# Sliding-window attention and two feed-forward layers on one core: both batches' first groups in packed float32, fewer chunks beside the attention, weight splits in step with the products

## The chip, the cores and the metric

One core of a Trainium2 chip runs the program. The metric is the time of one execution on the device in microseconds (us). Three runs of the kernel before gave 637.86, 638.09 and 638.39 us; the median is 638.09 us.

## What is computed

```python
scores = scale * np.matmul(q, k.transpose(0, 1, 3, 2))      # 2 batches, 8 heads, 768 rows, depth 64
keep = (pos[None, :] < n_sink) | ((rel >= 0) & (rel < window))   # n_sink 4, window 128
a = softmax(np.where(keep, scores, -1e9))
x = heads_side_by_side(np.matmul(a, v))                     # 1536 x 512
h = x @ w_in;  x = np.maximum(0.01 * h, h) @ w_out          # first layer, d_ff 2048
h = x @ w_in2; y = (h * sigmoid(h)) @ w_out2                # second layer, d_ff 2048
```

Everything is held to float32 accuracy. The products of the layers are made of three products of split operands (a high and a low part each).

## The kernel before

**Attention.** A unit is one group of 256 query rows (`G`, three groups in each of two batches) and one pair of heads (`p`, four pairs); there are 24 units, and each has two slots of 128 query rows. A slot goes through `scores` (PE makes the products `sc` for head 0 and head 1, DVE masks them into `P`, ACT takes the exponential and its row sum into `sm`), `normalise` (DVE forms the reciprocal of the sum, then `P` is multiplied by it: the first 16 slots on ACT, `ON_ACT`, the others on DVE), and `transposes` (PE transposes `P` with the identity matrix `ident` into `tr` or a bank lent by `h`, ACT copies it to `pT`). `values` multiplies by the values `v` into `at` (in places a bank lent by `ya`), and ACT and DVE split the result into `xh` and `xl`, the input of the layers. Groups after the first of a batch also carry the four sink columns (`psink`, `sink_t`, `sk`) and have 260 columns a head; the first group has 128 columns in slot 0 and 256 in slot 1.

The units of the first `WHOLE` = 2 groups (G = 0 and 1, both of batch 0) take the scores in plain float32, one head after the other; GpSimd fills the upper 64 partitions of their buffers with zeros once, and the loads bring 64 partitions. All later units split queries and keys in two parts first: ACT writes `qkh`, GpSimd `ql`, DVE the lower part of the keys.

**Layers.** `d_ff` is cut in 16 chunks of 128 for each layer. The first `NA` = 6 chunks of the first layer are done beside the attention, group by group, 256 columns wide: `item_h` makes `h` with 12 products, ACT and DVE make `ga` of it, `item_y` makes 12 products into `ya`. That is 36 items. The rest (chunks 6 to 15, and all of the second layer) comes after in passes of 4 and 6 chunks over the three blocks of 512 tokens (`T`), 512 columns wide (`fused_h`, `fused_y`): 78 items of 24 products.

**Weights.** They come as 64-bit words (`wr`), half a chunk in a transfer. `load_half` turns a half into a high and a low part: two ACT instructions (`wb`, `w` or `we`) and five DVE instructions.

**Order.** All of this is recorded first (`Recorder.add`), each instruction with an estimated cost and what it depends on; `Recorder.order` then plays the engines through with these costs and a due time, and issues each engine's instructions in the order that comes out. On the chip each engine keeps that order. The order in which the main loop asks for the work is the rank; `W_FIRST` and `W_EVERY` say from which slot on a half is asked for, and `go` which item goes with a slot.

Of the kernel before, what the change touches and what calls it, by code (L numbers as in the profile page):

```python
# [21 lines left out]
WHOLE = 2  # L22

NA, NE = 6, 4

AHEAD, FETCH = 2, 2

W_FIRST, W_EVERY = 1, 0.9

ON_ACT = 16  # L30
# [76 lines left out]
class Op:  # L107
    def __init__(self, eng, rank):
        self.eng, self.rank = eng, rank
        self.calls, self.cost, self.deps, self.opens, self.users = [], 0, {}, [], []  # L110
        self.bytes, self.port = 0, False


class Recorder:
# [27 lines left out]
    def cost(self, eng, name, out, ins, kw):  # L142
        n = out.size() if isinstance(out, View) else 0
        psum = any(isinstance(a, View) and a.tile.pool.psum for a in [out, *ins])
        if eng == "tensor":
            passes = 4 if ins[0].dtype == F32 else 1

            half = name == "matmul" and out.box[0][1] - out.box[0][0] <= 64
# [5 lines left out]
        if eng == "scalar":  # L154
            return (51 if psum else 93) + n / 1.2 + (186 if "accum_out" in kw else 0)
# [22 lines left out]
    def add(self, eng, name, args, kw):  # L178
# [18 lines left out]
        op.port = op.port or self.shared(eng, out, ins)  # L197
        op.cost += self.cost(eng, name, out, ins, kw)
        if name == "dma_start":
            side = writes[0] if writes else reads[0]  # L200
            op.bytes = 128 * side.size() * 4
        for views, write in ((reads, False), (writes, True)):
            for v in views:
                self.touch(op, v, write)

# [57 lines left out]
    def order(self):  # L263
# [6 lines left out]
        free = dict.fromkeys(self.ENGINES, 0.0)  # L270
        dma = port = 0.0
        ready = {e: [o for o in self.ops if o.eng == e and not o.need] for e in self.ENGINES}
# [27 lines left out]

        while len(done) < len(self.ops):
            best = None
            for e in self.ENGINES:
                can = []
                for o in ready[e]:
                    at = max(o.est, free[e], port if o.port else 0.0)
# [10 lines left out]
                if best is None or (start, o.due) < best[:2]:  # L317
                    best = (start, o.due, o)
            start, _, op = best
            op.start = start  # L320
            if op.bytes:
                free[op.eng] = start + (500 if op.eng == "sync" else 100)
                dma = max(dma, start + 1200) + max(op.bytes / 350.0, 370)
                end = dma + 300
            else:
                end = free[op.eng] = start + op.cost
                if op.port:
# [12 lines left out]
            for u in op.users:  # L340
                u.est = max(u.est, (op.start if not u.deps[op] else end + self.lag(op, u)))
                u.need -= 1
                if not u.need:
                    ready[u.eng].append(u)
# [45 lines left out]
def attention_moe(ctx, tc, cfg, ins, out):  # L390
# [141 lines left out]
    units = [(G, p) for G in range(B * NG) for p in range(NP)]  # L532
    state, sinks = {}, {}

    def load_qk(n):
# [5 lines left out]
        whole = G < WHOLE  # L541
        d = state[n] = dict(G=G, p=p, g=g, whole=whole, nb=2 if g == 0 else 3)
        raw = qk_raw[n % (4 if whole else 2)]

        rows = slice(0, D if n == 0 else P)
        load = slice(0, D if whole else P)
        for j in (slice(0, 1), slice(1, 2)) if n == 0 else (slice(0, 2),):
            R.sync.dma_start(out=raw[load, j, :GT + kw], in_=qkd[n][load, j, :GT + kw])
        if whole:
            d.update(q=[raw[rows]], k=raw[rows, :, GT:])  # L550
            return
        hi = attn.tile([P, 2, GT + 388], F32R, "qkh", 2)
# [7 lines left out]
    def load_v(n):  # L560
# [5 lines left out]
        R.sync.dma_start(out=d["v"][:, :nb], in_=vd[n][:, :nb])  # L566
# [14 lines left out]
    def scores(s):  # L581
# [9 lines left out]
        sm = attn.tile([P, 4], F32, "sm", 4)  # L591
        for j in range(2):
            sc = ps_a.tile([P, 260], F32, "sc", 2)
            with R.group():
                for a, q in enumerate(u["q"]):
                    R.tensor.matmul(sc[:, :nm], q[:, j, i * QB:(i + 1) * QB], u["k"][:, j, k0:k0 + nm],
                                    start=a == 0, stop=a == len(u["q"]) - 1)
# [6 lines left out]
    def normalise(s):  # L604
# [20 lines left out]
    def transposes(s):  # L625
# [101 lines left out]
    n_items = B * NG * NA  # L727
# [224 lines left out]
```

## Time and profile before

| | |
|---|---|
| time of the profiled execution | 638.0 us |
| its span (first to last instruction) | 636.0 us |
| median of three runs | 638.09 us |
| PE busy | 616.7 us (97%) |
| DVE busy | 406.3 us (64%) |
| ACT busy | 335.5 us (53%) |
| GpSimd (POOL) busy | 32.9 us (5%) |
| DMA | 54.39 MB |

The page shows the span in slices; a busy PE is one whose pipelined products leave no gap, not one at its peak. The granted TensorE clock of all slices is 1.0. How far a busy PE is from its pace is read from starts of products in the timeline. Tile names are the kernel's own; every instruction of the recorded part has the line of the issuing loop (L375 before), so that rows are told apart by tiles.

### The profile page before, as it was taken

The numbers are of one execution on the slowest core, as the hardware profiler recorded it, in microseconds if no ns is written. First come the engines' busy times: TensorE is split into PE (matmuls) and PEld (weight loads), VectorE is DVE, ScalarE is ACT, GpSimd is POOL, SyncE is SP. The second block draws the span as 40 slices with busy tenths as digits, with TensorE's granted clock in tenths as the row PEclk, the third lists the DMA queues.
The fourth block names the chain that finished last, engine by engine and source line by source line (L and its number), as shares of the span: only waits on it lengthen the run. The fifth ranks groups of instructions, "written<-read, shape, count | busy, mean of one in ns | idle before, by whom it ended". The sixth has DMA issues, their size and how long they took to land.

```text
span 636.0 us, 9261 instructions
## 1 busy us (share of the span) xinstructions
PE 616.7 (97%) x3392; PEld 521.4 (82%) x3392; DVE 406.3 (64%) x999; ACT 335.5 (53%) x802; POOL 32.9 (5%) x41
## 2 busy tenths in 40 slices
PE   7877899999999999999999999999999999999997
PEld 5566889999999888888888888888888888888886
DVE  4899989887649998693414999239542353333254
ACT  6999998898866654452323674356222242222221
POOL 5001112222000000000000000000000000000000
PEclk9999999999999999999999999999999999999999
DMA  8855535433003444142000343004100000000013
GB/s 223 230 170 179 174 117 189 157 111 109 26 1 133 166 165 164 46 155 99 2 0 1 118 148 113 20 1 146 54 0 1 0 1 0 1 1 1 1 66 132
DMA packets 19469, 54.39 MB, mean 86 GB/s; under 512 B 2144, under 2 KB 6496, under 8 KB 19424
## 3 DMA queue, kind: packets, MB, share of 16 engines
q1 hardware_dynamic: 19424, 53.81, 25.9%
q8 instruction: 26, 0.43, 0.3%
q14 instruction: 19, 0.16, 0.1%
HBM read 50.66 MB, written 3.15 MB: 85 GB/s over the span
## 4 chain that ended last, share of the span: by engine, by line
PE 85%; ACT 9%; DMA 2%; DVE 2%; issue 1%; SPq 0%; DVEq 0%; ACTq 0%
PE h L375 39%; PE y L375 33%; PE ya L375 5%; ACT P L375 4%; PE sc L375 3%; PE at L375 3%; PE tr L375 2%; DMA wr<-in_w 2%; ACT wb L375 1%; ACT w L375 1%; DVE wb L375 1%; ACT pT L375 1%; ACT qkh L375 1%; DMA qk<-in_qkd 0%; ACT ga L375 0%
## 5 line engine op out<-in xcount | busy, mean ns | idle before, releaser
L375 PE MATMUL h<-xh,w 128*128 128x512 f32 (+1 forms) x624 | 159.2, 344 | 1.6 <-ACT w L375 1.2
L375 ACT ACTIVATE g<-h 128x512 f32<-128x512 f32 (+1 forms) x114 | 60.1, 527 | 123.0 <-PE h L375 122.5
L375 PEld LDWEIGHTS h<-xh,w 128*128 128x128 f32 x624 | 107.6, 189 | 15.4 <-ACT w L375 1.4
L375 PE MATMUL h<-xl,w 128*128 128x512 f32 (+1 forms) x312 | 106.0, 340 | 0.0
L375 DVE TENSOR_TENSOR g<-g,h 128x512 f32<-128x512 f32 x48 | 32.9, 685 | 107.8 <-ACT g L375 107.8
L375 DVE TENSOR_TENSOR gb<-g,gb 128x512 fp32r<-128x512 f32 x78 | 53.7, 688 | 55.3 <-ACT g L375 34.8
L375 PE MATMUL h<-xh,we 128*128 128x512 f32 x288 | 88.6, 389 | 0.0
L375 DVE SCALAR_TENSOR_TENSOR wb<-wr,wb 128x512 uint32<-128x512 uint32 x128 | 86.5, 685 | 0.8
L375 PE MATMUL y<-we,gb 128*128 128x512 f32 x288 | 69.2, 389 | 0.0
L375 PE MATMUL y<-w,gb 128*128 128x512 f32 x288 | 68.9, 389 | 0.0
L375 PEld LDWEIGHTS h<-xl,w 128*128 128x128 f32 x312 | 58.9, 189 | 6.5
L375 PEld LDWEIGHTS y<-we,gb 128*128 128x128 f32 x288 | 54.0, 188 | 11.2
L375 PEld LDWEIGHTS y<-w,gb 128*128 128x128 f32 x288 | 54.0, 188 | 11.2
L375 PEld LDWEIGHTS h<-xh,we 128*128 128x128 f32 x288 | 54.0, 188 | 11.2
L375 ACT ACTIVATE P<-P,sm 128x260 f32<-128x260 f32 (+2 forms) x128 | 59.5, 485 | 5.0 <-DVE sm L375 4.4
L375 ACT ACTIVATE wb<-wr 128x512 f32<-128x512 f32 x64 | 43.1, 678 | 35.7 <-DMA wr<-in_w 20.9
L375 DVE TENSOR_SCALAR wb<-wb 128x512 f32<-128x512 f32 (+1 forms) x128 | 54.4, 430 | 7.5 <-ACT wb L375 5.7
L375 PE MATMUL ya<-ga,w 128*128 128x256 f32 x432 | 58.5, 284 | 0.1
L375 PE MATMUL h<-xl,we 128*128 128x512 f32 x144 | 56.0, 389 | 0.0
L375 PEld LDWEIGHTS ya<-ga,w 128*128 128x128 f32 x432 | 54.3, 190 | 1.0 <-issue 0.5
L375 PE MATMUL y<-gb,w 128*128 128x512 f32 x216 | 51.9, 389 | 0.0
L375 ACT ACTIVATE gb<-g 128x512 fp32r<-128x512 f32 x48 | 30.3, 632 | 34.4 <-DVE g L375 34.0
(68 smaller groups left out, 771.4 us busy)
## 6 DMA issues: line engine op xcount, KB each, us to landing
wr<-in_w SPq DMA_DIRECT2D x64, 512.0 KB, 3.8
qk<-in_qkd SPq DMA_DIRECT2D x12, 644.0 KB, 4.0
v<-in_vd SPq DMA_DIRECT2D x16, 192.0 KB, 3.7
out_y<-yp SPq DMA_DIRECT2D x11, 256.0 KB, 2.1
qk<-in_qkd SPq DMA_DIRECT2D x4, 512.0 KB, 4.3
v<-in_vd SPq DMA_DIRECT2D x8, 128.0 KB, 3.6
qk<-in_qkd SPq DMA_DIRECT2D x2, 322.0 KB, 8.2
qkh<-in_qkd SPq DMA_DIRECT2D x2, 322.0 KB, 7.9
```

The source lines that it names most:

```text
L375: getattr(eng, name)(*[_real(x) for x in a], **{k: _real(x) for k, x in kw.items()})
```

## The change

- The groups are taken in the order 0, 3, 1, 2, 4, 5 (`in_turn`): both batches' first groups, then the others. `WHOLE` is 3, so groups 0, 3 and 1 have plain float32 scores; splitting queries and keys falls away for group 3.
- The two heads of such a unit lie in partitions 0 to 63 and 64 to 127 (the layout on the host and `load_qk`); `scores` issues their two products together, on 64 partitions each, into the two `sc` buffers. GpSimd's zero fill goes.
- For the eight units of groups 0 and 3, `normalise` scales the identity by the reciprocal (`by`, 128 columns) instead of scaling `P`, and `transposes` multiplies `P` with `by` by an ordinary float32 product.
- A scaling is recorded with a choice of ACT, DVE or GpSimd (`either`, `scaled`); `order` takes the engine that would end it first. `ON_ACT` goes. The cost estimates are new.
- Beside the attention go 4, 5 and 6 chunks for the three blocks of tokens (`BESIDE`): 30 items in place of 36. The chunks left out come in the first pass, 15 items of 512 columns in place of 12.
- Halves are asked for every 1.3 slots in place of 0.9; in the passes a half is not issued before the `h` product recorded ahead of it.

```diff
-WHOLE = 2
+WHOLE = 3
+def in_turn(n_batches, n_groups):
+    return sorted(range(n_batches * n_groups), key=lambda G: (G % n_groups > 0, G))
+BESIDE = (4, 5, 6)
-W_FIRST, W_EVERY = 1, 0.9
-ON_ACT = 16
+W_FIRST, W_EVERY = 1, 1.3
...
+    def scaled(self, out, src, by, *more):
+        self.either(("scalar", "activation", (out, src, AF.Copy), dict(scale=by)),
+                    ("vector", "tensor_scalar", (out, src, by, None), dict(op0=ALU.mult)),
+                    ("gpsimd", "tensor_scalar", (out, src, by, 1.0), dict(op0=ALU.mult, op1=ALU.mult)))
...
-    units = [(G, p) for G in range(B * NG) for p in range(NP)]
+    turns = in_turn(B, NG)
+    units = [(G, p) for G in turns for p in range(NP)]
...
         if whole:
-            d.update(q=[raw[rows]], k=raw[rows, :, GT:])
+            raw = d["raw"] = qk_raw[n // 2 % 4][:, n % 2, :]
+            ends = (0, GT + P, GT + kw) if n == 0 else (0, GT + kw)
+            for a, e in zip(ends, ends[1:]):
+                R.sync.dma_start(out=raw[:, a:e], in_=qkd[G * NP + p][:, 0, a:e])
             return
...
+        if u["whole"]:
+            scs = {j: ps_a.tile([P, 260], F32, "sc", 2) for j in range(2)}
+            with R.group():
+                for j, sc in scs.items():
+                    r = slice(D * j, D * j + D)
+                    R.tensor.matmul(sc[:, :n], u["raw"][r, i * QB:(i + 1) * QB],
+                                    u["raw"][r, GT + k0:GT + k0 + n], start=True, stop=True)
...
+        if d["u"]["whole"] and d["g"] == 0:
+            d["by"] = attn.tile([P, 2, P], F32, "by", 3)
+            for j in range(2):
+                R.scaled(d["by"][:, j, :], ident, sm[:, 2 + j:3 + j])
+            R.bias = 0
+            return
         for j in range(2):
-            if s < ON_ACT:
-                R.scalar.activation(pt[:, j, :n], pt[:, j, :n], AF.Copy, scale=sm[:, 2 + j:3 + j])
-            else:
-                R.vector.tensor_scalar(pt[:, j, :n], pt[:, j, :n], sm[:, 2 + j:3 + j], None, op0=ALU.mult)
+            R.scaled(pt[:, j, :n], pt[:, j, :n], sm[:, 2 + j:3 + j])
...
-                    R.tensor.transpose(tr[:, o:o + P], pt[:, j, c * c1:c * c1 + P], ident)
+                    part = pt[:, j, c * c1:c * c1 + P]
+                    if "by" in d:
+                        R.tensor.matmul(tr[:, o:o + P], part, d["by"][:, j, :], start=True, stop=True)
+                    else:
+                        R.tensor.transpose(tr[:, o:o + P], part, ident)
...
+    beside = [(G, k) for G in turns for k in range(BESIDE[G * GT // 512])]
+    n_items = len(beside)
...
-        for t in (1, 2, 3, 0):
-            R.gpsimd.memset(qk_raw[t][D:], 0.0)
...
-            go = b >= OFF and m < (b - OFF + 1) * NA / (2 * NP)
+            G, k = beside[m] if m < n_items else (0, 0)
+            go = m < n_items and b - OFF + 1 > 2 * NP * (turns.index(G) + k / BESIDE[G * GT // 512])
...
+            starts = [min(BESIDE[T], c0) if c0 == NA else c0 for T in range(NT)]
+            items += [(layer, c, T, c == starts[T], c == c0 + n - 1, new, c0 + n == end)
+                      for T in range(NT) for c in range(starts[T], c0 + n)]
...
-            load_half()
+            load_half(R.at_h if f else None)
```

What moves shows best on the engines' own lists, in the issued order. A name's number counts the buffers handed out.

PE, the first rows of the attention (units 0 and 1; `sc` are scores, `tr` and `h` here hold transposed `P`). Before:

```order
L375 MATMUL sc_96<-qk_69 128x128
L375 MATMUL sc_108<-qk_69 128x128
L375 MATMUL sc_111<-qk_69 128x256
L375 MATMUL sc_119<-qk_69 128x256
L375 MATMUL sc_130<-qk_86 128x128
L375 MATMUL sc_138<-qk_86 128x128
L375 MATMUL sc_149<-qk_86 128x256
L375 MATMUL sc_162<-qk_86 128x256
L375 MATMUL tr_182<-ident_102,P_99 128x128 x2
```

and with the change:

```order
L441 MATMUL sc_110<-qk_69 128x128
L441 MATMUL sc_111<-qk_69 128x128
L441 MATMUL sc_134<-qk_69 128x256
L441 MATMUL sc_135<-qk_69 128x256
L441 MATMUL sc_153<-qk_69 128x128
L441 MATMUL sc_154<-qk_69 128x128
L441 MATMUL tr_170<-by_159,P_122 128x128 x2
L441 MATMUL sc_181<-qk_69 128x256
L441 MATMUL sc_182<-qk_69 128x256
L441 MATMUL h_187<-by_176,P_144 128x128 x4
```

The two scores of a slot now stand as a pair (neighbouring numbers), and the transposes read `by` and come earlier among the scores.

ACT at the same place (`P,sm<-P,sm` is the exponential, `P<-P,sm` the scaling). Before:

```order
L375 ACTIVATE P_99,sm_100<-P_99,sm_100 128x128 x2
L375 ACTIVATE P_122,sm_123<-P_122,sm_123 128x256 x2
L375 ACTIVATE P_140,sm_141<-P_140,sm_141 128x128
L375 ACTIVATE P_99<-P_99,sm_100 128x128 x2
L375 ACTIVATE P_122<-P_122,sm_123 128x256 x2
L375 ACTIVATE P_140,sm_141<-P_140,sm_141 128x128
L375 ACTIVATE pT_199<-tr_182 128x2x128
```

and with the change:

```order
L441 ACTIVATE P_122,sm_123<-P_122,sm_123 128x128 x2
L441 ACTIVATE P_144,sm_145<-P_144,sm_145 128x256 x2
L441 ACTIVATE P_164,sm_165<-P_164,sm_165 128x128
L441 ACTIVATE by_176<-ident_88,sm_145 128x128
L441 ACTIVATE P_164,sm_165<-P_164,sm_165 128x128
L441 ACTIVATE pT_192<-tr_170 128x2x128
L441 ACTIVATE P_195,sm_196<-P_195,sm_196 128x256 x2
```

Four scalings leave ACT here and one scaling of `ident` comes; the others of these `by` stand on DVE.

PE where the 256-column items end and the passes begin (`w` and `we` are split weights). Before:

```order
L375 MATMUL ya_7_2882<-ga_3013,w_888 128x256 x6
L375 MATMUL ya_5_2895<-ga_3013,w_888 128x256 x6
L375 MATMUL h_3061<-xh_0_282,we_2794 128x512 x2
L375 MATMUL h_3061<-xl_0_288,we_2794 128x512
L375 MATMUL h_3061<-xh_0_282,we_2794 128x512 x2
```

and with the change:

```order
L441 MATMUL ya_7_2675<-ga_2808,w_1831 128x256 x6
L441 MATMUL ya_5_2689<-ga_2808,w_1831 128x256 x6
L441 MATMUL h_2854<-xh_0_268,w_1070 128x512 x2
L441 MATMUL h_2854<-xl_0_292,w_1070 128x512
L441 MATMUL h_2854<-xh_0_268,w_1070 128x512 x2
```

The passes now begin with a chunk whose weights (`w`, chunk 4) were split during the attention.

## Rows read from the trace of the kernel before

**Rows 1.** Page, span in 40 slices: busy share in tenths.
```profile
PE   7877899999999999999999999999999999999997
ACT  6999998898866654452323674356222242222221
```
**Rows 2.** Windows, three stages: PE, PEld, DVE, ACT, POOL busy (count), clock, DMA.
```profile
0.00:71.00 71.00, 55.63 (x350) 41.89 (x350) 57.27 (x202) 64.60 (x196) 12.70 (x28) 1.00 0.70 203
71.00:187.00 116.00, 115.80 (x1002) 108.00 (x1003) 90.73 (x345) 98.16 (x309) 20.18 (x13) 1.00 0.33 107
187.00:636.00 449.00, 445.26 (x2046) 371.55 (x2042) 258.33 (x455) 172.74 (x299) 0.00 (x0) 1.00 0.18 61
```
**Rows 3.** Waits of PE from 15 to 75 us: total, times, longest.
```profile
PE tr L375 <- ACT P L375: 4.0, 5, 1.2
```
**Rows 4.** Timeline of DVE, ACT, PE: first mask, eighth `xh`, last values, last products.
```profile
4.32 0.29 DVE L375 CUSTOM_DVE_ANT_0 P<-sc,mask 128x128 f32<-128x128 f32 x1 [4.32 <-PE sc L375]
...
70.66 0.38 ACT L375 ACTIVATE xh<-at 128x256 fp32r<-128x256 f32 x1
...
186.22 1.09 PE L375 MATMUL at<-pT,v 128*64 128x256 f32 x12
...
629.66 2.65 PE L375 MATMUL y<-w,gb 128*128 128x512 f32 x11
```
**Rows 5.** ACT instructions by shape: count, busy us, mean ns, idle before.
```profile
L375 ACT ACTIVATE wb<-wr 128x512 f32<-128x512 f32 x64 | 43.1, 678 | 35.7 <-DMA wr<-in_w 20.9 <-DVE we L375 5.3 <-DVE w L375 4.4
L375 ACT ACTIVATE P<-P,sm 128x260 f32<-128x260 f32 x80 | 39.3, 507 | 0.7 <-DVE sm L375 0.4
L375 ACT ACTIVATE w<-wb 128x512 fp32r<-128x512 f32 x40 | 24.8, 627 | 14.9 <-DVE wb L375 10.1 <-PE y L375 4.6
L375 ACT ACTIVATE qkh<-qk 128x1288 fp32r<-128x1288 f32 x12 | 15.3, 1277 | 0.0
L375 ACT ACTIVATE P<-P,sm 128x128 f32<-128x128 f32 x24 | 9.0, 396 | 3.6 <-DVE sm L375 3.5
```
**Rows 6.** DVE instructions by shape, the same columns.
```profile
L375 DVE SCALAR_TENSOR_TENSOR wb<-wr,wb 128x512 uint32<-128x512 uint32 x128 | 86.5, 685 | 0.8
L375 DVE CUSTOM_DVE_ANT_0 P<-sc,mask 128x128 f32<-128x128 f32 x16 | 4.3, 290 | 6.0 <-PE sc L375 5.2 <-PE tr L375 0.7
L375 DVE TENSOR_SCALAR P<-P,sm 128x128 f32<-128x128 f32 x8 | 2.9, 409 | 0.0
```
**Rows 7.** Timeline of PE: start, us, form, count.
```profile
16.90 0.87 PE L375 MATMUL ya<-pT,v 128*64 128x256 f32 x8
17.70 0.44 PE L375 MATMUL tr<-ident,P 128*128 128x128 f32 x2
17.97 0.60 PE L375 MATMUL sc<-qk 128*128 128x260 f32 x2
18.41 0.62 PE L375 MATMUL h<-ident,P 128*128 128x128 f32 x4
18.87 0.60 PE L375 MATMUL sc<-qk 128*128 128x260 f32 x2
...
191.66 1.60 PE L375 MATMUL ya<-ga,w 128*128 128x256 f32 x12
193.10 0.40 PE L375 MATMUL h<-xh,w 128*128 128x256 f32 x2
```
**Rows 8.** Windows, inside a pass: columns as in rows 2.
```profile
300.00:350.00 50.00, 50.00 (x223) 41.39 (x222) 15.83 (x25) 15.24 (x27) 0.00 (x0) 1.00 0.00 1
```
**Rows 9.** Windows, two stretches with several engines full: columns as in rows 2.
```profile
30.00:60.00 30.00, 22.75 (x162) 17.73 (x160) 29.47 (x89) 29.74 (x88) 2.84 (x2) 1.00 0.56 184
60.00:80.00 20.00, 17.92 (x143) 16.14 (x144) 18.64 (x51) 17.98 (x52) 2.86 (x2) 1.00 0.49 162
```
**Rows 10.** DMA issues: count, KB each, median us to landing.
```profile
qk<-in_qkd SPq DMA_DIRECT2D x12, 644.0 KB, 4.0
qk<-in_qkd SPq DMA_DIRECT2D x2, 322.0 KB, 8.2
```

More of the change, by code (lines that the diff above doesn't have):

```diff
@@ L154, in cost @@
         if eng == "scalar":
-            return (51 if psum else 93) + n / 1.2 + (186 if "accum_out" in kw else 0)
+            by = any(isinstance(kw.get(k), View) for k in ("scale", "bias"))
+            sparse = isinstance(ins[0], View) and ins[0].tile.tag == "wr"
+            return (182 if by else 51 if psum else 93) + n / 1.2 + (95 if "accum_out" in kw else 55 if sparse else 0)
         if eng == "vector":
@@ L269, in order @@
         self.deadlines()
-        free = dict.fromkeys(self.ENGINES, 0.0)
+        free = dict.fromkeys(self.ENGINES, 700.0)
+        mode = None
         dma = port = 0.0
-        ready = {e: [o for o in self.ops if o.eng == e and not o.need] for e in self.ENGINES}
+        ready = {e: [o for o in self.ops if (o.eng == e or e in o.alts) and not o.need] for e in self.ENGINES}
         nxt = {(p, t): 0 for p in self.pools for t in p.tiles}
@@ L299, in opening, with later @@
             return at
+        def later(o, e):
+            if len(o.alts) < 2:
+                return False
+            end = max(o.est, free[e], port if o.alts[e][2] else 0.0) + o.alts[e][1]
+            for x, (_, cost, uses) in o.alts.items():
+                if x != e:
+                    first = sum(q.cost for q in ready[x] if q.due < o.due and not q.alts)
+                    if max(o.est, free[x] + first, port if uses else 0.0) + cost < end:
+                        return True
+            return False
         while len(done) < len(self.ops):
@@ L317, in order @@
                 if best is None or (start, o.due) < best[:2]:
-                    best = (start, o.due, o)
-            start, _, op = best
+                    best = (start, o.due, o, e)
+            start, _, op, eng = best
+            for e in op.alts:
+                if e != eng:
+                    ready[e].remove(op)
+            if op.alts:
+                op.eng = eng
+                op.calls, op.cost, op.port = op.alts[eng]
             op.start = start
@@ L322, in order @@
                 free[op.eng] = start + (500 if op.eng == "sync" else 100)
-                dma = max(dma, start + 1200) + max(op.bytes / 350.0, 370)
-                end = dma + 300
+                dma = max(dma, start + 1500) + max(op.bytes / 340.0, 370)
+                end = dma + 450
             else:
                 end = free[op.eng] = start + op.cost
+                if op.eng == "tensor":
+                    end = free[op.eng] = end + (95 if mode is not None and mode != op.mode else 0)
+                    mode = op.mode
                 if op.port:
@@ L802, in attention_moe @@
             load_chunk()
-    passes, items, c0 = [], [], NA
+    passes, counts, items, c0 = [], [], [], NA
     for layer, end in ((0, NCH), (1, 2 * NCH)):
@@ L810, in attention_moe @@
             new = layer == 1 and c0 == NCH
-            items += [(layer, c0 + k, T, k == 0, k == n - 1, new, c0 + n == end) for T in range(NT) for k in range(n)]
+            starts = [min(BESIDE[T], c0) if c0 == NA else c0 for T in range(NT)]
+            items += [(layer, c, T, c == starts[T], c == c0 + n - 1, new, c0 + n == end)
+                      for T in range(NT) for c in range(starts[T], c0 + n)]
+            counts.append(len(items) - sum(counts))
             c0 += n
     due, n0 = [], 2 * NA
-    for n, nxt in zip(passes, passes[1:] + [0]):
+    for n, m_p, nxt in zip(passes, counts, passes[1:] + [0]):
         n0 += 2 * n
-        due += [n0 + 2 * nxt * (i + 1) / (NT * n) for i in range(NT * n)]
+        due += [n0 + 2 * nxt * (i + 1) / m_p for i in range(m_p)]
     while m < n_items + 2:
```

77 lines of the change are left out of this document (52 added, 25 removed).

## The prediction

> **What bounds the kernel now.** I read four views. The page's slices first [rows 1]: PE is at seven or eight tenths in the first five slices and at nine from there to the last but one, while ACT is full in the second to fifth and falls off later. So two things make the time: how long the first 75 us take with a PE that is not full, and how many products PE has to get through after. The windows of three stages say it in numbers [rows 2]. I cut at the eighth copy to `xh` (the eighth unit, 70.7 us), at the end of the last value product (186.22 + 1.09 = 187.3 us) and at the end of the last product of all (629.66 + 2.65 = 632.3 us) [rows 4]; 3.7 us of output follow. Stage 1 (to 70.7) has PE busy 55.6, DVE 57.3 and ACT 64.6 us; stage 2 (116.6 us) has PE 115.8 of 116 busy; stage 3 (445.0 us) is PE alone, DVE at 58% and ACT at 38%. That ACT sets stage 1 is seen in 30 to 60 us, where ACT has 29.74 and DVE 29.47 of 30 [rows 9], and in PE's waits, whose largest in that stretch is the transposes' for ACT's `P`, 4.0 us [rows 3]. Something gained on ACT or DVE in stage 1 therefore counts; in stages 2 and 3 only PE work counts, as long as ACT does not fill up.
>
> **Paces.** Busy time of PE overlaps, so its prices are distances between starts. Twelve 256-column products take 193.10 - 191.66 = 1.44 us, 0.12 each; two float32 score rows of 260 columns (one plain product is two rows) take 18.41 - 17.97 = 0.44; four transposes 18.87 - 18.41 = 0.46, 0.115 each [rows 7]; a 512-column product 50 / 223 = 0.224 [rows 8]. On ACT and DVE the means [rows 5, 6] hold an overlap with the next instruction: the list of stage 1 before, count times mean, comes to 81.5 us for ACT where 64.6 are busy (0.79), and to 68 for DVE where 57.3 are (0.84). I work out differences by means and scale them so.
>
> **Stage 1, the first eight units.** They were groups 0 and 1; now they are groups 0 and 3, which have no sinks and fewer columns; group 1 moves to stage 2.
> - ACT loses 32 scalings (16 of 260 columns at 0.507, the others 0.40 to 0.50: 15.3 us) and gains 7 `by` at 0.396 and one scaling, 3.3. It loses three `qkh` at 1.277 (3.8) [rows 5], four halves of weights (four `wb` at 0.678 and four `w` at 0.627: 5.2), 23 small sink copies at about 0.2 (5.2), two items (four copies, 1.5), and 3 by the narrower exponentials and `pT` copies. Net 31; times 0.79, ACT falls from 64.6 to 40 us.
> - DVE gains 21 `by`. Their form has no row; between the 128-column mask at 0.29 and the 128-column scaling at 0.409 ([rows 6]; one with a wait in it) I take 0.29: 6.1 us, at most 8.6. It loses four halves at two `wb` of 0.685, two of 0.43 and one `w` of 0.685 (11.6), two key splits of 0.97, 1 on masks and 4 on sinks and items. Net -12.4; times 0.84, from 57.3 to 46.9 us.
> - PE loses two items (48 products of 0.12, 5.8 us) and about 6 on scores and values, and gains 48 `by` products in place of transposes at 0.22 (two rows of 128 columns at half the price of 260) against 0.115, 5: from 55.6 to some 48 busy, under 53. So the doubled price of a transpose is covered here by the wait for DVE; without that cover it would cost 5 us.
> - GpSimd loses four zero fills and gains four `by`; nothing waits for them.
>
> DVE is the fullest now. It starts at 4.3 us [rows 4], needs 46.9, and from its last mask to the unit's `xh` are an exponential, a transpose, a copy and the values, some 2 us: **stage 1 is 53 us** (49 if lists overlap better, 59 if the first units are held up), 17.7 less.
>
> **Stage 2, the other sixteen units.** PE: four items fewer (96 products of 0.12, -11.5). Group 1 stands here in place of group 3: its scores are 8 pairs. The row nearest to a pair is that of the values, where two heads fill the two halves of the array's columns: eight rows take 17.70 - 16.90 = 0.80 us [rows 7], where one after the other they would take 1.29 by the 0.44 above, and half of it is 0.65; so halves do run together, at some 0.15 extra for a group. A pair is then 0.44 + 0.15, eight of them 4.7, against 32 split products, 3.8. Three more transposes a unit (1.4) and longer value products (12 rows for 8 and a sink product, 0.4 a unit, 1.6) come to +4 in all. PE needs 116.6 - 7.5 = 109 us. No row shows two halves of rows, though, only of columns. The Trainium skill (TensorEngine Tiling (Array Packing), Gotcha 1: PSUM Pressure) says that row tiles write to different PSUM banks and cannot use one bank at the same time; if the two `sc` buffers shared a bank, the pairs would run one after the other and PE would need 8 x 0.44 = 3.5 us more, 112.5. No run here shows which; it is rival 2.
>
> ACT: it takes over what stage 1 sheds. 21 scalings of 260 columns (10.6), four more halves (5.2), group 1's sinks (5.2), wider exponentials (2.3), less four items (3.0): +20.7; times 0.79 to 0.81 on 98.2 busy gives 115 us; packed without any gap 112.6. DVE gets 3.9 more on its list, 94 us. So ACT passes PE: 113 to 115 against 109, and each waits for the other (scores before the exponentials, exponentials before the transposes). From 30 to 60 us two engines stood at 98 and 99% together [rows 9], so two full engines need not cost much. I take **115 us**, 1.6 less than before; ends 109 and 124.
>
> **Stage 3.** The same number of items is left over (95 `ya` products in both). Three items of 512 columns come: 72 products of 0.224, +16.1, so **461.1 us**. Weights: the first passes now begin with chunks split long before, which gives the first new chunk 11 us more than it had; the later ones are asked for later, but counted in products each still stands some 50 us of PE work or more ahead of its use in the issued order. DVE at 58% and ACT at 38% cover it; price nothing. If that cover failed, PE would wait before a pass's first `h`.
>
> **The sum.** 53 + 115 + 461.1 + 3.7 = 632.8 against 636.0 of span; the profiled execution has 638.0, 2.0 more than its span, and 638.0 is 0.1 below the median of the runs. Forecast: **635 us**, 3 less. Of the 19 us off stages 1 and 2, 16 come back as products in stage 3. A measurement of this kernel tells about 0.2% (1.3 us) from no change, so the line is at 636.8 and 639.3 us.
>
> **Rivals.**
> 1. ACT packs its list and stage 2 stays PE's: 109 to 110 us, time 629 to 630. For it: in the old stage 2 PE was at 115.8 of 116 with ACT at 98.2, 85% [rows 2]; against it, 113 to 115 is more than 109.
> 2. The pairs do not run together, that is the change does not do what it says on PE: 112.5 for PE beside ACT's 113 to 115, which I put at 118, time 638. The 5 us more in stage 1 are covered.
> 3. Slower: ACT and PE, equally loaded, trade waits through all of stage 2, because a slot's scores need both `sc` buffers free and PE stands in line behind an item. From 60 to 80 us, the one stretch with three engines near full, the fullest had 18.64 of 20 and PE and ACT 18 [rows 9]. ACT's 115 at 93% is 123 us, time 643; at 90% 128. It decides from a stage 2 of 119.4 on.
> 4. The first units are held up. Before, a load on 64 partitions took 8.2 us where one of twice the size on 128 took 4.0 [rows 10]; the new ones are on 128, which speaks against. But the loads that stand in the list up to the fourth unit sum to 6.6 MB, for 26 us, and stage 1 moved 203 GB/s with the queues 70% busy [rows 2], 5.3 MB. At 59 us of stage 1 the time is 641.
>
> **How the numbers follow.** Forecast 0.43, rivals 0.20, 0.12, 0.17 and 0.08. Faster by over 0.2%: nearly all of the forecast, rival 1 and a quarter of rival 2, 0.61. Within: the rest of the forecast, most of rival 2 and the edges of 3 and 4, 0.16. Slower: rivals 3 and 4, 0.23. The range is 627 to 644 us: below it lies a better mesh than rival 1, above it the 90% case of rival 3. The forecast's own cases lie from 632 to 638.
>
> **What would show it.** In the changed profile the eighth `xh` copy starts near 53 us and the last value product ends near 168; DVE is full up to the first, ACT above 95% from there to the second, and PE has waits for ACT in that stretch where it had none. Two rows of a score pair should start within some 0.01 us of each other; 0.22 apart would be rival 2. The rest should be 461 us of PE without a gap. The forecast is wrong if stage 2 is under 111 or over 119, if stage 1 passes 57, or if PE waits for weights in the passes.

## The result, and the profile after

The changed kernel takes **629.4 us** (median of four runs, 628.87 to 630.64) against 638.19 us of the kernel before (637.86 to 638.39): a ratio of 0.9867, 95% interval 0.9855 to 0.9879, 8.8 us faster by the medians and 1.3% by the ratio. The profiled execution took 629.62 us with a span of 627.8. The forecast was 635.0 us, faster, with a range of 627 to 644: the sign is right, the range holds, and two thirds of the gain were missed.

The page's slices of PE and ACT, which answer to [rows 1]:

```profile
PE   7899999999999999999999999999999999999997
ACT  5989999999764333332434256454323323332221
```

ACT is at nine tenths from the fourth slice to the tenth, where it fell to eight tenths after the sixth before, and PE is at nine tenths from the third slice on and not from the sixth. The windows, cut at the eighth `xh` copy and at the end of the last value product, with the columns of [rows 2]:

```profile
0.00:49.80 49.80, 44.07 (x309) 33.35 (x310) 41.02 (x185) 39.85 (x128) 5.61 (x25) 1.00 0.62 206
49.80:163.20 113.40, 111.65 (x949) 100.32 (x949) 91.42 (x343) 109.78 (x356) 23.82 (x19) 1.00 0.41 137
163.20:628.00 464.80, 461.01 (x2112) 385.17 (x2112) 268.23 (x458) 171.05 (x305) 0.00 (x0) 1.00 0.17 59
```

The cuts themselves are rows of the timeline of ACT and of PE, as in [rows 4]; the last products of all start at 620.65 and last 3.56 us, so stage 3 ends at 624.2:

```profile
49.81 0.39 ACT L441 ACTIVATE xh<-at 128x256 fp32r<-128x256 f32 x1 [0.23 <-PE at L441]
...
162.10 1.09 PE L441 MATMUL at<-pT,v 128*64 128x256 f32 x12
...
620.65 3.56 PE L441 MATMUL y<-w,gb 128*128 128x512 f32 x15
```

| us | before | forecast | after | miss |
|---|---|---|---|---|
| stage 1, to the eighth `xh` copy | 70.7 | 53 | 49.8 | -3.2 |
| stage 2, to the last value product | 116.6 | 115 | 113.4 | -1.6 |
| stage 3, the passes | 445.0 | 461.1 | 461.0 | -0.1 |
| output | 3.7 | 3.7 | 3.6 | -0.1 |

So 24.1 us came off the first two stages and 16.0 came back in the third. Shorter windows of the changed kernel show who is full where:

```profile
0.00:15.00 15.00, 10.97 (x49) 7.55 (x49) 7.02 (x45) 8.43 (x27) 3.80 (x21) 1.00 0.87 294
15.00:30.00 15.00, 13.87 (x110) 10.40 (x108) 14.64 (x69) 14.52 (x50) 1.44 (x3) 1.00 0.49 158
30.00:45.00 15.00, 14.43 (x113) 11.39 (x114) 14.93 (x58) 13.41 (x44) 0.37 (x1) 1.00 0.52 169
...
100.00:120.00 20.00, 19.55 (x166) 17.45 (x165) 15.82 (x61) 19.87 (x65) 5.68 (x6) 1.00 0.36 125
120.00:140.00 20.00, 19.64 (x170) 18.54 (x169) 15.86 (x55) 19.83 (x65) 7.94 (x5) 1.00 0.36 112
```

From 15 to 45 us DVE is busy 29.57 us of 30; from 100 to 140 ACT is busy 39.70 us of 40, with PE close behind. In the first 15 us no engine is full, so that DVE is not full all the way to the eighth `xh` copy, as was forecast: over stage 1 it has 41.02 us of 49.8. PE's waits over the whole span (total, times, longest) answer to [rows 3]; the transposes' 4.0 us for ACT's `P` are gone, and nothing large took their place:

```profile
PE sc L441 <- DMA qk<-in_qkd: 3.2, 1, 3.2
PE sc L441 <- DVE sm L441: 1.3, 4, 0.5
PE tr L441 <- ACT pT L441: 1.2, 1, 1.2
PE at L441 <- ACT sink_t L441: 1.0, 3, 0.4
```

### The profile page after: what moved, and what is told of

Its sections match the earlier page's. It is cut to its first block, busy times and chain, and to the rows that moved or that the text cites. A ratio compares the mean times of both kernels' runs of the same rounds, so it can differ in the third digit from the quotient of the medians.

```text
span 627.8 us, 9200 instructions
## 1 busy us (share of the span) xinstructions
PE 616.7 (98%) x3368; PEld 518.8 (83%) x3368; DVE 400.7 (64%) x984; ACT 320.7 (51%) x789; POOL 29.4 (5%) x44
## 4 chain that ended last, share of the span: by engine, by line
PE 87%; ACT 10%; DVE 2%; issue 1%; DMA 0%; DVEq 0%; ACTq 0%
PE h L441 40%; PE y L441 35%; PE ya L441 5%; ACT P L441 4%; PE sc L441 3%; PE tr L441 2%; PE at L441 2%; ACT pT L441 2%; ACT qkh L441 1%; DVE P L441 1%; ACT psink L441 1%; ACT sink_t L441 1%; ACT ga L441 0%; ACT xh L441 0%; DMA qk<-in_qkd 0%
## 5 line engine op out<-in xcount | busy, mean ns | idle before, releaser
L441 PE MATMUL h<-xh,w 128*128 128x512 f32 (+1 forms) x600 | 157.2, 350 | 0.0
L441 PEld LDWEIGHTS h<-xh,w 128*128 128x128 f32 x600 | 104.7, 189 | 14.7 <-issue 0.8
L441 DVE TENSOR_TENSOR gb<-g,gb 128x512 fp32r<-128x512 f32 x81 | 55.9, 690 | 77.0 <-ACT g L441 61.2
L441 ACT ACTIVATE gb<-h 128x512 fp32r<-128x512 f32 x33 | 19.7, 597 | 100.9 <-PE h L441 100.9
L441 PEld LDWEIGHTS h<-xl,w 128*128 128x128 f32 x300 | 56.7, 189 | 7.1
L441 ACT ACTIVATE P<-P,sm 128x260 f32<-128x260 f32 (+2 forms) x118 | 56.8, 492 | 7.5 <-DVE sm L441 7.3
L441 PE MATMUL y<-gb,w 128*128 128x512 f32 x252 | 60.5, 389 | 0.0
L441 PEld LDWEIGHTS y<-gb,w 128*128 128x128 f32 x252 | 47.3, 188 | 9.8
L441 PE MATMUL ya<-ga,w 128*128 128x256 f32 x360 | 49.6, 286 | 0.0
L441 DVE TENSOR_TENSOR yp<-yp,y 128x512 f32<-128x512 f32 (+1 forms) x61 | 38.0, 673 | 14.7 <-PE y L441 14.7
```

Of the source, the lines that this page charges most:

```text
L441: getattr(eng, name)(*[_real(x) for x in a], **{k: _real(x) for k, x in kw.items()})
```

## The experiments

Every kernel ran beside runs of the kernel before, whose median was 637.1 to 638.2 us; where kernels are compared with one another, their ratios to it are used.

### Do the two heads of a pair run together?

In the changed kernel's trace the rows of a pair start 6 or 7 ns apart (16.032 and 16.039, 16.246 and 16.252 us). The next kernel takes that away: both heads use partitions 0 to 63, so that head 1's scores are made from head 0's data.

```diff
-                    r = slice(D * j, D * j + D)
+                    r = slice(0, D)
```

> Head 1's scores are made from head 0's data in partitions 0 to 63 for the 12 packed units (so head 1's result is another one), which puts both products of a pair on the same rows of the array: they must run one after the other. Order and everything else are the same. PE work: 16 slots of groups 0 and 3 at 0.22 and 0.43 us (5.2), 8 of group 1 at 0.44 (3.5). If DVE sets stage 1 and ACT stage 2, most is covered: time up by 1 to 4 us. If PE sets them, up by 7 to 9. If pairs did not overlap in the changed kernel, no change.

651.03 us (one run), 21.6 more than the changed kernel, 19.3 of it in stage 1 (69.1 us). The pairs are worth something, but not this much: the rest is TensorE's clock. The kernel's timeline of PE at 29 us and a window of it:

```profile
28.65 1.22 PE L441 MATMUL sc<-qkh 64*128 64x128 f32 x4
29.80 1.22 PE L441 MATMUL tr<-by,P 128*128 128x128 f32 x4
...
15.00:45.00 30.00, 30.00 (x112) 21.59 (x111) 16.65 (x73) 17.31 (x53) 1.44 (x3) 1.00 0.24 77
```

PE is busy all 30 us and has 112 rows; the changed kernel had 223 in the same 30. Four `tr` rows (two plain float32 products of two rows each) stretch over 1.22 us where they take 0.71 later in the changed kernel. That is the lower of the two clock levels (1.2 GHz), and it lasted to 46.6 us, from where the record of the granted clock shows 1.0. (The clock column says 1.00 in the window above as there is no record before; the starts of the products tell.) Stage 2, at full clock throughout, was 115.5 us, 2.1 more: that is what the pairs are worth there. What they are worth in stage 1 cannot be told apart from the clock.

### Who sets the first 50 us, and who the next 113?

Five kernels keep every instruction of the changed kernel in its order and double or leave out one kind. First DVE in stage 1: head 1's masking is issued twice with the same values (`m_dve`), or the addition of 1e-9 to the sum is left out, which changes no value (`y_eps0`).

```diff
+            if s < 16 and j:
+                R.ops[-1].calls *= 2
```

> Head 1's mask instruction is issued twice in the first 16 slots (the second writes the same values), in places where the planner counts no cost: 8 of 128 columns and 8 of 256, with their sum reads 5.8 us of DVE by starts of rows. If DVE holds stage 1 from 15 us on, the eighth xh copy moves from 49.8 to 55 to 56 us and the time rises by 5 to 6. If PE or the chain from one unit to the next holds it, the copy comes before 52 and the time rises by less than 2.

632.49 us (one run); DVE is busy 5.2 us more in stage 1 and stage 1 is 52.6 us, between the two cases of the expectation.

```diff
         R.vector.tensor_scalar(sm[:, 2:4], sm[:, 2:4], 1.0e-9, None, op0=ALU.add)
+        R.ops[-1].calls = []
```

> The addition of 1e-9 is left out again (it changes no value, since the sum is at least 1), but now with every other instruction on every engine in the changed kernel's own order: 48 instructions fewer on DVE, and no list is made anew. 16 of them stand in stage 1, 0.163 us each, 0.09 after the 0.07 by which a DVE row overlaps the next: 1.4 us. Theory A, DVE's list sets stage 1: stage 1 is 48 to 48.8 us and the time 627.5 to 628.5. Theory B, not DVE: 629 to 630. If A holds, the 631.7 us of the kernel with the list made anew is the work of the new list and not of the instruction.

630.56 us (628.28 to 630.99; ratio 0.9884, 0.9865 to 0.9903), no gain that can be told, and stage 1 of the profiled execution was 51.1 us, *longer* by 1.3. Read alone, that is theory B and worse. The same stretch of the other kernels that share the order of stage 1 says something else. PE's timeline of the changed kernel, then of `y_hi2` (below; it differs in stage 2 alone):

```profile
9.63 2.08 PE L441 MATMUL h<-by,P 128*128 128x128 f32 x8
11.63 0.80 PE L441 MATMUL sc<-qk 64*128 64x128 f32 x4
12.36 1.22 PE L441 MATMUL tr<-by,P 128*128 128x128 f32 x4
13.51 0.70 PE L441 MATMUL sc<-qk 64*128 64x256 f32 x4
14.14 0.87 PE L441 MATMUL at<-pT,v 128*64 128x256 f32 x8
14.94 1.16 PE L441 MATMUL h<-by,P 128*128 128x128 f32 x8
16.03 0.49 PE L441 MATMUL sc<-qk 64*128 64x128 f32 x4
16.45 0.71 PE L441 MATMUL tr<-by,P 128*128 128x128 f32 x4
```

```profile
9.65 1.72 PE L441 MATMUL h<-by,P 128*128 128x128 f32 x8
11.30 0.49 PE L441 MATMUL sc<-qk 64*128 64x128 f32 x4
11.72 0.71 PE L441 MATMUL tr<-by,P 128*128 128x128 f32 x4
```

The same four `tr` rows take 1.22 us in one execution and 0.71 in the other: the clock rises at a moment that differs from execution to execution, and stage 1 with it.

| profiled execution of | record of full clock from | stage 1 |
|---|---|---|
| `y_hi2` | 10.9 us | 48.7 us |
| `m_pe` | 11.6 | 49.0 |
| the changed kernel | 13.5 | 49.8 |
| `m_act` | 17.5 | 51.7 |
| `m_dve` (DVE +5.2 busy) | 11.5 | 52.6 |
| `y_eps0` (DVE -1.0 busy) | 17.2 | 51.1 |

Among the first four, which issue the same stage 1, 6.6 us of later rise cost 3.0 us. Beside the kernels with nearly the same rise, `m_dve` is 3.6 us longer and `y_eps0` 0.5 shorter. So DVE sets stage 1 from the point where it is full: 70% of what is put on it comes out as a longer stage. Half of what is taken off comes back, but 0.5 us between two single profiles is little to rest on.

Then stage 2: the second slot's `pT` copy on ACT issued twice (`m_act`), one small sink copy on ACT left out, so that one part of the sink product is zero (`y_hi2`), and four transposes on PE issued twice (`m_pe`).

```diff
         R.scalar.activation(u["pT"][:, :, (i + 1) * 256 - n:(i + 1) * 256],
                             tr[:, 0:2 * n].rearrange("p (j n) -> p j n", j=2), AF.Copy)
+        if s >= 16 and i:
+            R.ops[-1].calls *= 2
```

> In the units from the eighth slot pair on, one copy of pT on ACT a slot is issued twice with the same values: 16 copies of 0.48 us, 7.7 us more on ACT in stage 2, nothing on PE or DVE. Theory A, ACT sets stage 2: it grows by 6 to 8 us and the time to 635.5 to 637.5 us, ACT 116 to 118 us busy there. Theory B, PE sets it and ACT has room: stage 2 can grow only by what ACT exceeds PE's 112 us, 4 us at most, and the time is 631 to 633.5 us.

```diff
             R.scalar.activation(hi2, hi, AF.Copy)
+            R.ops[-1].calls = []
```

> In the changed kernel's own order the second copy of the sinks' high part on ACT is left out, so that this part of the sink product is zero: 32 copies of 0.19 us, about 0.1 each by starts, 3.2 us off ACT, all in stage 2; nothing moves. Theory A, ACT sets stage 2: stage 2 is 110 to 111 us and the time 626 to 627. Theory B, PE sets it: 113 us and 629 to 630. Theory C, the two stand in each other's way and only a part comes back: 111.5 to 112.5 and 627.5 to 628.7.

```diff
                         R.tensor.transpose(tr[:, o:o + P], part, ident)
+        if s >= 16 and i:
+            R.ops[-1].calls *= 2
```

> In the changed kernel's own order the four transposes of the second slot of each unit in stage 2 are issued twice with the same values: 64 of 0.115 us, 7.4 us more on PE, nothing elsewhere. The same on ACT (16 copies, about 8 us) made stage 2 9.6 us longer. Theory A, ACT sets stage 2 and PE has the 1.8 us that it is idle: 118 to 119.5 us, time 634 to 635.5. Theory B, PE sets it: 120.5 to 121.5, time 636.5 to 637.5. Theory C, PE's and ACT's work alternate in a chain: as B or more.

Windows over stage 2 of `m_act`, `y_hi2` and `m_pe`:

```profile
51.60:174.60 123.00, 114.77 (x951) 100.83 (x949) 92.25 (x345) 119.52 (x373) 23.25 (x19) 1.00 0.38 127
```

```profile
48.70:160.50 111.80, 111.50 (x949) 100.11 (x949) 90.61 (x343) 106.60 (x324) 23.84 (x19) 1.00 0.42 139
```

```profile
49.00:165.50 116.50, 116.50 (x1013) 106.86 (x1013) 91.05 (x343) 110.86 (x357) 23.36 (x19) 1.00 0.41 133
```

ACT doubled: it is busy 9.7 us more and stage 2 is 123.0 us, 9.6 longer, more than theory A had; the time is 641.09 (one run), of which a late rise of the clock has 1.9 in stage 1. ACT less 3.2: stage 2 is 111.8, half of it gained, and the time 628.26 (ratio 0.9857, 0.9837 to 0.9878), theory C. PE doubled: 64 transposes 0.109 us apart are 7.0 us, and stage 2 is only 3.1 longer, 632.09 us: less than every theory. It tells something that no busy share did: with 7.0 us added PE runs through 116.5 us without a wait in its record, so PE's own work in stage 2 is 116.5 - 7.0 = **109.5 us**, although the window of the changed kernel shows it busy for 111.65; a row's modelled end reaches over short waits. Starts of rows bear this out: the 947 steps from one row to the next, each taken at its shortest in six executions with this order (the changed kernel, `m_pe`, `m_act`, `m_dve`, `y_eps0` and `y_hi2`), add to 109.1 us. ACT sets stage 2 there (109.8 of 113.4, 97%), in that work put on it counts in full, and PE stands 4 us behind. The doubled copies and the doubled transposes belong to the same 16 slots, so a mere chain from transposes to copies would have been lengthened by both.

### One part undone

Without the normalising products (`if False:` in place of the condition on `d["u"]["whole"]`):

> P is scaled as before also in groups 0 and 3 (by the engine that the planner takes), and transposed by the identity. Counts: in stage 1 ACT has 1.8 us more, DVE 0.8 less, PE 5 less. If DVE and ACT hold the attention, the time stays within 2 us of the changed kernel. If PE held stage 1, it is 3 to 5 us faster. If normalising in the transposing products was what brought the gain, it is 4 us or more slower.

631.43 us (ratio 0.9895, 0.988 to 0.991). Stage 1 is 49.6 us and stage 2 115.4: the loss stands in stage 2, where neither kernel has normalising products. Six chunks beside all blocks (`BESIDE = (6, 6, 6)`):

> Six chunks beside the attention everywhere, the rest as changed: 36 items and 12 items in the first pass. Stage 1's DVE list grows by 9.7 us, PE has 17.3 us more to do up to the last value product and 16.1 less after it. By the theory that DVE sets stage 1 and the fuller of ACT and PE stage 2: eighth copy near 59, last value product near 178 us, time 627 to 631, the same within 2 us as the changed kernel. If the fewer chunks are what brought the gain, 633 or more.

629.29 us (0.9869, 0.9851 to 0.9886), no difference from the changed kernel, with stage 1 at 58.2 us and stage 2 at 120.5: the fewer chunks of the changed kernel take 15.5 us off these two and give 16.3 back in the passes. Groups in their natural order, so that only group 0 has normalising products and group 2 is packed in place of group 3:

> Groups in their natural order again (0, 1, 2 packed, so group 3 is split as before; `by` for group 0 alone). Counted in starts of rows, stage 1 has 5.0 us more DVE and 7.7 more ACT than the changed kernel, the attention as a whole 0.8 less ACT, 1.8 less PE. By the theory (stage 1 by DVE, stage 2 by the fuller of ACT and PE) stage 1 is 55, stage 2 106 to 108, time 627 to 630: the order of the groups brings nothing by itself. If taking both first groups first is what brought the gain: 633 or more.

631.98 us (0.9907, 0.9882 to 0.9931), against the expectation; stages 1 and 2 are 57.2 and 109.8 us, both some 2 us or more above it. Two whole groups (0 and 3) in place of three:

> Groups 0 and 3 packed, group 1 split in two parts as in the kernel before. ACT has 2.5 us more and DVE 6.0 more in the attention, PE 0.4. By the theory 630 to 632. If keeping a third group from being split brought the gain: 634 or more.

631.54 us (0.9898, 0.9874 to 0.9922), as expected.

### Parts alone

The recorder's choice of engine and its new costs, in the kernel before:

> The kernel before with the new planner alone (its costs, and the choice of engine for a scaling); everything else as before, no packed pairs. ACT's list in stage 1 falls from 62.4 to 56.0 us by starts of rows, DVE's rises from 54.6 to 57.7, GpSimd takes some scalings; PE's work is the same as before, 152.9 to the end of the attention. By the theory that ACT set the old stage 1: stage 1 64 to 65, time 631 to 633. If the packed pairs carry the gain: within 1.5 us of the kernel before.

635.51 us (0.9964, 0.9951 to 0.9977), less than half of the gain that was expected. With the packed pairs as well (two whole groups, natural order, six chunks, no normalising products):

> From the change only the packed pairs (groups 0 and 1), the planner's new costs and its choice of engine for a scaling: natural order, two whole groups, no `by`, six chunks everywhere. Stage 1 has 57.5 us of DVE and 54.5 of ACT by starts (before: 54.6 and 62.4, of ACT too much). By the theory stage 1 falls from 70.7 to 64, stage 2 stays at PE's 116, time 630 to 632: most of the 8.8 us gained. If the gain comes from the groups' order, `by` or the chunks: 636 or more.

637.25 us (0.9991, 0.9982 to 1.0001): a miss, and 1.7 us slower than without the pairs. The same with fewer chunks:

> Packed score pairs and the new choice of engines with the fewer chunks beside attention, but in the natural order of units, two groups whole and no normalising products. The same with six chunks took 637.25 us. Theory A, chunks beside attention are neutral because their products return one for one in stage 3 as 512-column products: 636 to 638 us, stages 1 and 2 together 18 to 21 us shorter and stage 3 16 us longer. Theory B, fewer chunks free DVE and ACT where they set stage 1: 629 to 632 us, stage 1 at 55 to 58 us.

636.71 us (0.9989, 0.9975 to 1.0003), stages 1 and 2 together 16.3 us shorter and the rest 16.3 longer: theory A, and the second time that the number of chunks beside the attention makes no difference. In these three kernels the clock falls to its lower level near 50 to 62 us. Two windows of the second of them, ahead of the fall and in it, and the row of PE's timeline just before the fall:

```profile
50.00:55.00 5.00, 2.45 (x17) 1.90 (x15) 4.94 (x10) 4.46 (x13) 1.71 (x1) 1.00 0.63 208
55.40:58.60 3.20, 3.15 (x14) 2.84 (x14) 2.78 (x12) 2.81 (x8) 0.00 (x0) 0.50 0.50 168
```

```profile
55.14 0.46 PE L441 MATMUL sc<-qkh 128*128 128x260 f32 x1 [2.46 <-DVE sm L441]
```

PE was busy for half of the 5 us ahead of it and had just waited 2.46 us for DVE, which was full (4.94 of 5): here the fall comes after the wait for DVE and not before it. Is the lower clock what ate the gain? Each pair was issued twice:

```diff
+            if s < 16:
+                R.ops[-1].calls *= 2
```

> The packed pairs and the new choice of engines alone (637.25 us), and in the first sixteen slots each score pair is issued twice with the same values: some 7 us more of PE work in a stage 1 in which PE was busy 57.9 of 70.3 us. Theory A, the lower clock from 55 to 59 us and the late rise at 21 us are what ate the gain of the pairs, and they come from a PE with too little to do there: the clock rises earlier and does not fall, stage 1 is 66 to 68 us in spite of the added work, and the time is 633 to 635.5 us. Theory B, the clock is a by-product and the lists of DVE and ACT set stage 1: it stays at 70 us and the time at 637 us. Theory C, PE's time counts there: 73 us or more and 640 us.

639.6 us (1.0034, 1.002 to 1.0047). The clock rose at 13.8 us in place of 21.2, and stage 1 was 71.4 us in place of 70.3; the fall stayed (54.8 to 61.6 us). Theory A is down, and the result lies between B and C: the earlier rise did not pay for the added work, in a kernel in which both DVE (59.0 us) and ACT (57.5) are loaded in stage 1. What the rise alone is worth is not shown, as 7 us of PE work came with it. No kernel takes the fall away, but its price can be read from the kernel before: of its 55 executions beside these kernels, 29 had a mean granted clock of 0.996 or less (a fall of 6.8 us makes 0.995) and a median of 638.2 us, 22 had 1.0 and 637.1. So a fall goes with some 1.1 us, far less than the 6 to 8 that separate these kernels from the changed one.

### Work taken off, with the lists made anew

Three kernels take work from an engine and let the recorder order everything afresh: no scaling of `P` on ACT; besides, head 1's normalising diagonal always on GpSimd; and the addition of 1e-9 not recorded at all.

> The scaling of P that stands in units without the normalising products may go to DVE or GpSimd only, not to ACT. ACT loses 8.8 us of its list up to the end of attention, DVE gains 6.4, PE's list is the same. Theory A, ACT sets stage 2 of the changed kernel (109.8 us busy of 113.4): stage 2 falls to about 110 us, by no more than PE's own 109 to 110 allows, and the time to 626 to 627 us. Theory B, PE sets stage 2 (111.65 us busy of 113.4): ACT drops to about 103 us busy, stage 2 stays at 113 and the time at 629 to 630 us. Against both: scalings on GpSimd beside DVE lengthen DVE's rows to 1 to 2 us, and the time rises to 631 us.

> As the kernel without scalings on ACT, and the diagonal of each unit with normalising products is made for head 0 on DVE and for head 1 on GpSimd. By the lists DVE has 42.1 and ACT 37.0 us in stage 1, and 131.6 and 131.8 to the end of attention (changed kernel 134 and 143 by the same count). Theory A, ACT sets stage 2 and DVE stage 1: stage 1 falls to 47 to 49 us, stage 2 to 110, the time to 624 to 627 us. Theory B, PE sets stage 2 and GpSimd only stretches DVE's rows: 629 to 632 us.

> The addition of 1e-9 to the sum of exponentials is left out. Since the row's maximum gives exp(0) = 1, the sum is at least 1 and the addition changes no float32 value. It is 48 instructions of 0.163 us on DVE, 17 of them in stage 1 (2.8 us by durations, about 1.5 by starts), and one step less in each slot's chain. Theory A, DVE's list sets stage 1 of the changed kernel: stage 1 is 47.8 to 48.8 us and the time 627.5 to 628.7. Theory B, stage 1 is set by the chain from loads to PE and not by DVE: stage 1 as before, 629 to 630 us. In stage 2 DVE is busy 91 of 113 us and a gain there is only that of the chain.

630.25 us (0.9889, 0.9865 to 0.9912), 631.96 (0.9914) and 631.7 (0.9907, 0.9892 to 0.9923): the first cannot be told from the changed kernel, the others are slower. In the first ACT fell to 103.3 us busy in stage 2, and stage 2 did not shorten (114.2), while DVE rose from 91.4 to 100.5. So ACT's list is the bound in the changed kernel's order, but taking work from it in another order does not free the stage; what holds that order at 114 us was not found. The third differs from `y_eps0` only in its order; its clock rose at 14.0 us, and its stage 1 is 51.6 us where the changed kernel with a rise at 13.5 has 49.8. So a new list alone costs 1 to 2 us: 1.7 by these two profiles, 1.5 by the ratios (0.9907 and 0.9884), whose intervals still touch. A fourth, the third without scalings of `P` on GpSimd, came to 632.08 us (0.9915), as its theory B had it:

> As the kernel without the addition of 1e-9, and the scalings of P may go to DVE or ACT only, not to GpSimd, where they took 0.48 to 1.06 us and stood beside DVE rows of 1 to 2 us. The normalising diagonals may still go to all three. Theory A, what GpSimd does to DVE's rows costs stage 2 time: 111 to 112.5 us there, time 626 to 628. Theory B, PE and ACT at 98 and 97% set stage 2 and DVE's long rows are covered: the same as the kernel without the addition alone, within 1 us.

What GpSimd's rows do to DVE's is seen in the changed kernel itself, in the timelines of DVE and GpSimd:

```profile
137.89 2.10 DVE L441 TENSOR_TENSOR qkh<-qk,qkh 64x776 fp32r<-64x776 f32 x1
```

```profile
137.87 1.29 POOL L441 TENSOR_TENSOR ql<-qk,qkh 128x512 fp32r<-128x512 f32 x1 [5.04 <-issue]
```

The key split takes 2.10 us beside `ql` where the twelve of stage 2 have a mean of 1.127. DVE has 22 us of room in stage 2, which covers it.

No kernel tried here beats the changed one by more than its interval, not even `y_hi2` (0.9857 against 0.9867), which leaves work out.

## Why the forecast was right and where it was wrong

**The step that failed** is in "Paces": "count times mean, comes to 81.5 us for ACT where 64.6 are busy (0.79), and to 68 for DVE where 57.3 are (0.84). I work out differences by means and scale them so." The sums of the lists came out right. The forecast had 68 - 12.4 = 55.6 us on DVE in stage 1, and the rows of the changed kernel sum to 55.0; for ACT in stage 2 it added 20.7 to rows that sum to 121.0, 141.7, and they sum to 142.4. But the overlap is not a share of a list; it is an amount for each instruction that stands behind another. Where an engine is full it is the same before and after:

| | rows | sum of rows | busy | overlap of one row |
|---|---|---|---|---|
| DVE before, 30 to 60 us | 88 | 35.9 us | 29.5 us | 0.073 us |
| DVE after, stage 1 | 185 | 55.0 | 41.6 | 0.073 |
| ACT before, 30 to 60 us | 87 | 37.5 | 29.6 | 0.091 |
| ACT after, stage 2 | 356 | 142.4 | 109.8 | 0.092 |

(These are the rows that start in the stretch, and the busy times are their union, so that one may differ from a window's by half a microsecond.) As shares, the same rows give 0.82 and 0.76 for DVE, 0.79 and 0.77 for ACT, so that DVE's tell the two readings apart. With [rows 9] read in this way the forecast's own lists give DVE 55.6 - 185 x 0.073 = 42.1 us and ACT 141.7 - 356 x 0.091 = 109.3, where it took 46.9 and 113 to 115. The list of stage 1 became one of shorter rows (0.30 us in the mean for 0.35: 21 `by` of 0.28, no key splits), so a share read from the old list understated the overlap.

Not all of DVE's 5.3 us are the overlap's. The old rows sum to 69.9 us and not to 68, so that 14.9 went and not 12.4; the two slips cancel in the new list, but at 0.84 the difference makes 2.1 of the 5.3, and the overlap 3.2. Smaller slips carry nothing: ACT's five terms in stage 2 add to 20.3 and not to 20.7, 23 sink copies at 0.2 are 4.6 and not 5.2, the 112.6 of ACT packed without a gap has no working, and in [rows 1] ACT's nines reach to the sixth slice.

By the forecast's own further steps (4.3 to start, 2 to the unit's end) 42.1 us make stage 1 48.4; it was 49.8, of which the clock's rise holds about 1 (stage 1 was 48.7 in `y_hi2`, whose clock rose 2.6 us earlier).

**A second step failed in stage 2 and hid the first.** "Two full engines need not cost much" was read from DVE and ACT. ACT and PE, which need 109.8 and 109.5 us, take 113.4 together, so they cost each other 3.6. ACT's need was put 3 to 5 us too high and this price at nothing; that 115 was only 1.6 us off is luck. Rival 1 is right by its condition (ACT at 109.3 beside PE's 109), and its 629 to 630 us is what came, but by luck too: its stage 2 of 109 to 110 us did not come and did not become PE's, as `m_act` against `m_pe` shows, and the time came because stage 1 was 3.2 us shorter than it assumed.

**What held.** PE's need in stage 2, forecast 109, is 109.5 by `m_pe`. ACT in stage 1, forecast 40 us, had 39.85. Stage 2 stayed between 111 and 119 us and stage 1 under 57. The pairs run together: 7 ns apart, and a 256-column pair takes 14.14 - 13.51 = 0.63 us with its way in and out, where 0.59 was taken from the values' rows [rows 7]. Rival 2 falls with that. The Trainium skill (TensorEngine Tiling (Array Packing), Gotcha 1: PSUM Pressure) says that row tiles cannot use one PSUM bank at a time; the two `sc` buffers lie in banks of their own in the changed program (4 and 5) and their rows run together, and no run here put them in one. The doubled price of a transpose, 0.22 us, is what the rows have (two rows 0.111 apart), and most of it is covered where DVE is full: without these products (`u_no_by`) stage 1 is 49.6 us with a rise of the clock at 16.4 us, which by the table above is worth some 1.3, so that at most 1.5 of the 5 us come through, by one profile with another list. The 72 products of 512 columns cost stage 3 16.0 us for the 16.1 of the sum. The later halves of weights never made a pass wait, and the constant 1.3 is no cause: with 0.9 in its place every engine's list comes out the same. The rule that holds a half back in the passes was not tried alone. Of GpSimd's four `by`, for which nothing was to wait, one held PE up for 0.4 us.

**The rivals.** Rival 3, ACT and PE trading waits at 90 to 93%, fell as it was priced: ACT is at 97% in stage 2, and the waits cost the 3.6 us above, not 8 or more. Rival 4 fell: PE waits for a load once, 3.2 us at the start. No rival spoke of TensorE's clock, though it moves stage 1 by up to 3 us between executions; the rows of before that it read, from 16.90 us on [rows 7], are all at full pace.

**What the parts are worth** is settled only in part. Undone one at a time, the number of chunks is worth nothing, and by the ratios the normalising products, the third whole group and the new order of groups are worth 1.8, 2.0 and 2.6 us each. But `x_noeps`, which only leaves work out, is 2.6 us slower with its list made anew, and the loss of `u_no_by` stands in stage 2, where it changed nothing but the list. So a margin of 2 us can be the part's or its list's. What stands: the choice of engines and its new costs alone bring 2.3 us of the 8.8; with none of the three other parts the packed kernels are at 0.9989 and 0.9991 of before, and with any two of the three at 0.9895 to 0.9907. The three margins add to 6.4 of the 7.8 us between `s_chunks` and the changed kernel, so no large gain is left that only the whole has, if they are the parts' own. Why the packed pairs alone are slower than the choice of engines alone (637.25 against 635.51) stays open.

## What to carry to other kernels

Sums of row durations overstated a full engine by a fixed time for each row here (0.073 us on DVE, 0.091 on ACT), not by a share: read that time from a stretch where the engine is full, and subtract it times the count. To learn what an engine really needs, issue some of its work twice in the same order and see from where the stage grows; a busy share of 98% hid 4 us on PE here. When two engines come out equally full, give their waits for each other a price; here it was 3.6 us of 113. Where a program orders the work, test a part with the order held fixed, or the new order is what gets measured.

## What was not expected of the hardware

- TensorE's clock came up at 10.9 to 17.5 us in executions of one and the same order, and the 1.8 us between the changed kernel's runs are no more than that can make. With both heads on the same 64 partitions it stayed at its lower level to 46.6 us, though PE was busy for 30.00 of 30 us. In `s_packed` it fell again (55.3 to 58.7 us) right after one wait of PE of 2.46 us.
- Going from products on the whole array to halves of rows and back costs time at each turn: the last row of a group of `by` products is followed by a 128-column pair after 0.205 us, the pair by `tr` after 0.201, where 128-column rows stand 0.111 apart. The second row on either side is late as well (0.214 us after the first, in the pair and in `tr`), so that there and back costs some 0.4 us.
